# A decode block of attention and gated ReLU: gating before the up and down rows are loaded, and products moved to VectorE

## Chip, cores and metric

The kernel runs on 1 core of one Trainium2 chip. The metric is the device time of one execution in microseconds, as the median of 3 runs. Everything is in 32-bit floats.

## What is computed

One token `x` of 576 numbers is normalized, and attention over a cache of 8192 positions with 32 heads of 128 is added to a gated feed-forward part, both of the same normalized token. Only `x` is small: K and V are 134 MB each, and each of `wq`, `wo`, `W_gate`, `W_up` and `W_down` is 9.4 or 10.6 MB. Each is used once.

```python
D, H, Sk, Dh, F = 576, 32, 8192, 128, 4608

xn = _layernorm(x, axis=-1)

# attention
q = (xn @ wq).reshape(B, 1, H, Dh).transpose(0, 2, 1, 3)
scores = jnp.einsum("bhqd,bhkd->bhqk", q, k_cache) * (Dh ** -0.5)
p = _softmax(scores, axis=-1)
o = jnp.einsum("bhqk,bhkd->bhqd", p, v_cache)
a = o.transpose(0, 2, 1, 3).reshape(B, 1, H * Dh) @ wo

# gated feed-forward
gate = jnp.einsum("bsd,df->bsf", xn, W_gate)
up = jnp.einsum("bsd,df->bsf", xn, W_up)
gate = gate * (gate > 0)
h = gate * up
b = jnp.einsum("bsf,fd->bsd", h, W_down)

return x + a + b
```

Where a gate is not positive, `h` is zero, and neither that column of `W_up` nor that row of `W_down` has a part in the output. The inputs are drawn from a normal distribution with a fixed seed.

## The kernel before

All weights and the cache pass once through a pool of five buffers, `st`, of up to 32 KB on each of the 128 partitions (`NST`, line 25, and line 34). The helper `stream` (line 40) takes a buffer and issues the load; a load can start when the tile that was in its buffer is used up. Most loads are issued by SyncE (SP); every second K tile is issued by ScalarE (`nc.scalar if i % 2 else nc.sync` in `scores`), so two queues carry K and one carries the rest.

The order of work is the order of the program on each engine:

- Line 47 to 89: constants, the normalized `xn` on one partition, and its transposition onto the partitions by six small products into `px`, copied to `xz`. `xz` and `qz` are zero but for one column in 63, so that a window of 32 columns of them puts a product's result into one chosen row of a 32-row block.
- `project` (line 91) multiplies `xn` by a weight matrix on TensorE, with the matrix as the moving side, in five steps of contraction (line 107). It is used for `wq` before everything else, and the result is turned and copied into `qz`.
- For each of four groups of eight heads (`NG`, `G`): `scores` streams eight K tiles of 4 MB, transposed beforehand, and makes one 128 x 512 tile of scores (line 139). `softmax` (line 143) takes maxima and exponentials and turns the result into `pT`. `values` streams eight V tiles of 4 MB (line 180); for each head, VectorE copies the result out of PSUM (`oc`, line 183), and eight matmul instructions add up its four blocks into one column of `ot` (line 185). At the end of the group `os` gets the group's eight output columns.
- `gate_up` is called in the last group between `softmax` and `values`: `project` for `W_gate`, then the ReLU on VectorE (lines 192 and 193), `project` for `W_up`, the product of both, and its turning into `hh`.
- The end: `rows` multiplies a block of 128 rows of `wo` or `W_down` by a column of `os` or `hh` and adds to `acc` (line 218): 32 blocks of `wo` in four loads of eight, then 36 of `W_down` in loads of 8, 8, 8, 6, 4, 1 and 1. Each block is four products of 144 columns, each into another quarter of the partitions. `x` is added, and the 576 numbers are stored.

A 32-bit matmul of the program is two instructions in the trace, so 16 products of a head count 32.

Of the kernel before, what the change touches and what calls it, by code (L numbers as in the profile page):

```python
# [8 lines left out]

F32 = mybir.dt.float32  # L10
AF = mybir.ActivationFunctionType
ALU = mybir.AluOpType
AX = mybir.AxisListType

P = 128
D = 576
H = 32
SK = 8192
DH = 128
F = 4608  # L20
FC = F // P
G = 8
NG = H // G
EPS = 1e-5
SCALE = DH ** -0.5
NST = 5
Q = D // 4


@with_exitstack  # L30
def tile_block(ctx: ExitStack, tc: tile.TileContext, x, kt, vt, wq, wqt, wg, wu, wgt, wut, wo, wd, out):
    nc = tc.nc
    cp = ctx.enter_context(tc.tile_pool(name="cp", bufs=1))
    st = ctx.enter_context(tc.tile_pool(name="st", bufs=NST))
    wk = ctx.enter_context(tc.tile_pool(name="wk", bufs=2))
    pk = ctx.enter_context(tc.tile_pool(name="pk", bufs=2, space=bass.MemoryType.PSUM))
    pv = ctx.enter_context(tc.tile_pool(name="pv", bufs=1, space=bass.MemoryType.PSUM))
    ps = ctx.enter_context(tc.tile_pool(name="ps", bufs=2, space=bass.MemoryType.PSUM))

    def stream(src, queue=nc.sync):  # L40
        n = src.shape[-1]
        t = st.tile([P, n], F32, tag="st", name="st")
        queue.dma_start(t, src)
        return t


    xr = cp.tile([1, D], F32, name="xr")
    nc.scalar.dma_start(xr, x)
    ident = cp.tile([P, P], F32, name="ident")
    make_identity(nc, ident)  # L50

    hs = cp.tile([P, G], F32, name="hs")
    nc.vector.reduce_sum(hs, ident.rearrange("p (j i t) -> p i j t", j=4, i=G), axis=AX.XY)
    sb = cp.tile([P, 4], F32, name="sb")
    nc.vector.reduce_sum(sb, ident.rearrange("p (j m) -> p m j", j=4)[:, :4, :], axis=AX.X)

    x4 = cp.tile([P, Q], F32, name="x4")
    nc.gpsimd.memset(x4, 0.0)
    nc.scalar.dma_start(x4[0:P:32, :], x.rearrange("o (j q) -> (o j) q", j=4))

    one = cp.tile([1, 1], F32, name="one")
    nc.vector.memset(one, 1.0)
    eps = cp.tile([1, 1], F32, name="eps")
    nc.vector.memset(eps, EPS)
    qz = cp.tile([P, H, 63], F32, name="qz")
    nc.gpsimd.memset(qz, 0.0)
    po = [pv.tile([P, 512], F32, name=f"po{i}") for i in range(2)]
    for t in po:
        nc.vector.memset(t, 0.0)


    sm = cp.tile([1, 8], F32, name="sm")
    xn = cp.tile([1, 6 * P], F32, name="xn")
    sq = cp.tile([1, D], F32, name="sq")
    nc.vector.memset(xn, 0.0)
    nc.vector.reduce_sum(sm[:, 0:1], xr, axis=AX.X)
    nc.vector.tensor_scalar_mul(sm[:, 1:2], sm[:, 0:1], 1.0 / D)
    nc.vector.tensor_scalar(sq, xr, sm[:, 1:2], None, op0=ALU.subtract)
    nc.scalar.activation(xn[:, :D], sq, AF.Square, accum_out=sm[:, 2:3])
    nc.scalar.activation(sm[:, 3:4], sm[:, 2:3], AF.Sqrt, bias=eps, scale=1.0 / D)  # L80
    nc.vector.reciprocal(sm[:, 4:5], sm[:, 3:4])
    nc.vector.tensor_scalar_mul(xn[:, :D], sq, sm[:, 4:5])  # L82
    nc.vector.tensor_copy(xn[:, 704:768], xn[:, 512:576])
    px = ps.tile([P, 8], F32, tag="sm", name="px")
    for a in range(6):
        nc.tensor.matmul(px[:, a:a + 1], xn[:, a * P:(a + 1) * P], one, start=True, stop=True)  # L86
    xz = cp.tile([P, 6, 63], F32, name="xz")
    nc.gpsimd.memset(xz, 0.0)
    nc.vector.tensor_copy(xz[:, :, 31], px[:, :6])

    def project(w, wt, slots, n):

        tt = stream(wt)
        pr = pk.tile([P, 512], F32, tag="pk", name="pr")
        for b in range(slots // 4):
            r = b
            for a in range(5):
                if a % 2 == 0 and a < 4:
                    t = stream(w[b, a // 2])
                for j in range(4):  # L100
                    s = 4 * b + j
                    second = s >= slots // 2
                    if a < 4:
                        col, rhs = a, t[:, (a % 2 * 4 + j) * n:][:, :n]
                    else:
                        col, rhs = 4 + second, tt[:, (s % (slots // 2)) * n:][:, :n]
                    nc.tensor.matmul(pr[32 * j:32 * j + 32, :n], xz[:, col, 31 - r:63 - r], rhs,  # L107
                                     start=(b == 0 and a == 0), stop=(s >= slots - 4 and a == 4))
        return pr

    def turned(rows, n):

        m = n // P
        pt = ps.tile([P, 4, P], F32, tag="sm", name="pt")
        for b in range(m):
            nc.tensor.transpose(pt[:, b, :], rows[:, b * P:(b + 1) * P], ident)  # L116
        return pt


    pq = project(wq, wqt, 8, 512)  # L120
    qr = wk.tile([P, 512], F32, tag="p", name="qr")
    nc.vector.tensor_copy(qr, pq)
    pqt = turned(qr, 512)
    for r in range(2):
        nc.vector.tensor_copy(qz[:, 16 * r:16 * r + 16, 31].rearrange("d (j b) -> d j b", b=4),
                              pqt.rearrange("d b (j r) -> d j b r", r=32)[:, :, :, r])

    os = cp.tile([P, H], F32, name="os")

    def scores(g):  # L130
        s = pk.tile([P, 512], F32, tag="pk", name="s")
        for i in range(G):
            h = G * g + i
            t = stream(kt[h], nc.scalar if i % 2 else nc.sync)
            for u in range(4):
                r = 4 * i + u
                for j in range(4):
                    c = (4 * u + j) * 512
                    nc.tensor.matmul(s[32 * j:32 * j + 32, :], qz[:, h, 31 - r:63 - r], t[:, c:c + 512],  # L139
                                     start=(r == 0), stop=(r == 31))  # L140
        return s

    def softmax(g, s):
# [26 lines left out]
    def values(g, pT, rl):  # L170
        ot = ps.tile([P, G], F32, tag="ot", name="ot", bufs=1)
        for i in range(G):
            h = G * g + i
            o = po[h % 2]
            t = stream(vt[h])
            for u in range(4):
                for j in range(4):
                    row = 32 * j + 4 * i + u
                    c = (4 * u + j) * 512
                    nc.tensor.matmul(o[32 * j:32 * j + 4, :], pT[:, row, :], t[:, c:c + 512],  # L180
                                     start=(u == 0), stop=(u == 3))
            oc = wk.tile([P, 512], F32, name="oc")
            nc.vector.tensor_copy(oc, o)  # L183
            for b in range(4):
                nc.tensor.matmul(ot[:, i:i + 1], oc[:, b * P:(b + 1) * P], sb[:, b:b + 1],  # L185
                                 start=(b == 0), stop=(b == 3))
        nc.vector.tensor_mul(os[:, G * g:G * g + G], ot, rl)

    def gate_up():
        pg = project(wg, wgt, 12, 384)  # L190
        gr = wk.tile([P, 512], F32, tag="p", name="gr")
        nc.vector.tensor_scalar(gr[:, :384], pg[:, :384], 0.0, None, op0=ALU.is_gt)
        nc.vector.tensor_mul(gr[:, :384], gr[:, :384], pg[:, :384])
        pu = project(wu, wut, 12, 384)
        nc.vector.tensor_mul(gr[:, :384], gr[:, :384], pu[:, :384])
        ph = turned(gr, 384)
        hh = cp.tile([P, 3, P], F32, name="hh")
        nc.vector.tensor_copy(hh, ph[:, :3, :])
        return hh

    for g in range(NG):
        s = scores(g)
        pT, rl = softmax(g, s)
        if g == NG - 1:
            hh = gate_up()
        values(g, pT, rl)


    acc = pk.tile([P, 512], F32, tag="pk", name="acc")
    nc.vector.memset(acc[:, :Q], 0.0)  # L210
    total = H + FC
    done = 0

    def rows(t, i, col):
        nonlocal done
        for j in range(4):
            c = i * D + j * Q
            nc.tensor.matmul(acc[32 * j:32 * j + 1, :Q], col, t[:, c:c + Q],  # L218
                             start=(done == 0), stop=(done == total - 1))
        done += 1  # L220

    for b in range(4):
        t = stream(wo[b])
        for i in range(8):
            rows(t, i, os[:, 8 * b + i:8 * b + i + 1])
    f = 0
    for n in (8, 8, 8, 6, 4, 1, 1):
        t = stream(wd[:, f * D:(f + n) * D])
        for i in range(n):
            s, b = divmod(f, 3)  # L230
            r = 32 * (s % 4) + s // 4
            rows(t, i, hh[:, b, r:r + 1])
            f += 1
    res = cp.tile([P, Q], F32, name="res")
    nc.vector.tensor_add(res, acc[:, :Q], x4)
    nc.sync.dma_start(out.rearrange("o (j q) -> (o j) q", j=4), res[0:P:32, :])
# [40 lines left out]
```

## Time and profile before

| | |
|---|---|
| runs | 754.05, 753.93, 753.52 us; median 753.93 us |
| profiled execution, first to last instruction | 751.8 us |
| mean granted TensorE clock | 0.761 |
| read from HBM | 319.16 MB |
| DMA issues of K / V | 32 / 32, 4096 KB each |

No time beyond its span is listed for the profiled execution. In the profile's names PE is TensorE, PEld its weight loads, DVE VectorE, ACT ScalarE, POOL GpSimd, SP SyncE, and a q behind a name is the engine's instruction queue. A row of a group reads: line, engine, operation, result<-operands, shapes, count | busy us, mean ns of one | idle time of the engine just before, and what ended it. A row of the DMA issues reads: result<-source, issuing queue, operation, count, KB of one, and median us from issue to landing. In the list of DMA queues a row has the packets, the MB and the time that the packets took as a share of 16 engines' span. In the chain of waits the work that ended last is followed back from its end.

### The profile page before, as it was taken

The page shows a single profiled execution, that of the slowest core. Times are in us where ns is not written, and L with a number is a line of the kernel's source. Part 1 is how long each engine was busy: PE and PEld are TensorE (multiplying, and loading weights), DVE is VectorE, ACT ScalarE, POOL GpSimd, SP SyncE. Part 2 cuts the span into 40 slices and gives each one's busy share as a digit, 9 for nine tenths or more (in the row PEclk, how much of TensorE's full clock was granted, in tenths as well). Part 3 has the DMA queues.
Part 4 walks back from the last instruction along what each step waited for, and adds up shares of the span by engine and source line. Part 5 has one row for each costly group of instructions (what it writes and reads, how often), then busy time and mean ns, then how long its engine had stood idle before and what let it go on. Part 6 is the DMA issues. An engine that isn't in the chain of part 4 may idle for free.

```text
span 751.8 us, 6828 instructions
## 1 busy us (share of the span) xinstructions
PE 422.7 (56%) x3223; PEld 129.3 (17%) x3223; DVE 40.3 (5%) x87; ACT 8.0 (1%) x14; POOL 2.9 (0%) x9
## 2 busy tenths in 40 slices
PE   4353467663463576636445677443745645766755
PEld 2010012211110121101111222111111211221333
DVE  2000001000000010000000100000000100000000
ACT  1000000000000000000000000000000000000000
POOL 1000000000000000000000000000000000000000
PEclk9677788876776797667686776766867997787777
DMA  9999999999999999999999999999999999999996
GB/s 377 432 445 418 445 418 438 425 436 428 432 432 431 433 427 437 425 439 420 439 425 438 425 437 428 432 432 431 433 428 404 415 429 441 424 440 420 429 426 291
DMA packets 13581, 319.60 MB, mean 425 GB/s; under 512 B 1513, under 2 KB 1521, under 8 KB 1778
## 3 DMA queue, kind: packets, MB, share of 16 engines
q1 hardware_dynamic: 11240, 252.06, 78.4%
q10 hardware_dynamic: 2314, 67.11, 20.8%
q8 instruction: 25, 0.41, 0.2%
q14 instruction: 2, 0.02, 0.0%
HBM read 319.16 MB, written 0.00 MB: 425 GB/s over the span
## 4 chain that ended last, share of the span: by engine, by line
DMA 62%; PE 25%; another core or an unknown queue 10%; DVE 2%; issue 0%; ACT 0%; SPq 0%; ACTq 0%
DMA st<-in_kt 26%; DMA st<-in_vt 24%; PE po L180 10%; PE s L139 10%; DMA st<-in_wo 4%; DMA st<-in_wd 3%; DMA st<-in_wu 2%; DMA st<-in_wg 1%; PE pr L107 1%; PE ot L185 1%; DMA st<-in_wq 1%; PE acc L218 1%; DVE oc L183 1%; PE pt L116 0%
## 5 line engine op out<-in xcount | busy, mean ns | idle before, releaser
L180 PE MATMUL po<-st,pT 128*4 128x512 f32 x1024 | 176.4, 851 | 95.6 <-DMA st<-in_vt 93.7
L139 PE MATMUL s<-st,qz 128*32 128x512 f32 x1024 | 139.8, 708 | 140.3 <-DMA st<-in_kt 140.3
L139 PEld LDWEIGHTS s<-st,qz 128*32 128x32 f32 x1024 | 34.9, 128 | 242.0 <-DMA st<-in_kt 142.8
L180 PEld LDWEIGHTS po<-st,pT 128*4 128x4 f32 x1024 | 29.8, 108 | 213.0 <-issue 114.7
L107 PE MATMUL pr<-st,xz 128*32 128x384 f32 (+1 forms) x320 | 38.1, 603 | 32.2 <-DMA st<-in_wq 14.0
L185 PE MATMUL ot<-sb,oc 128*128 128x1 f32 x256 | 33.7, 253 | 26.3 <-DVE oc L183 26.3
L185 PEld LDWEIGHTS ot<-sb,oc 128*128 128x128 f32 x256 | 31.0, 191 | 58.1 <-DVE oc L183 58.1
L183 DVE COPY oc<-po 128x512 f32<-128x512 f32 x32 | 22.1, 691 | 302.5 <-PE po L180 302.5
L107 PEld LDWEIGHTS pr<-st,xz 128*32 128x32 f32 x320 | 9.9, 120 | 57.5 <-DMA st<-in_wq 17.6
L145 DVE TENSOR_REDUCE mr<-s 128x1 f32<-128x512 f32 x4 | 2.8, 691 | 279.5 <-PE s L139 279.5
L218 PE MATMUL acc<-st,hh 128*1 128x144 f32 x288 | 12.8, 344 | 8.6 <-DMA st<-in_wd 8.6
L218 PE MATMUL acc<-st,os 128*1 128x144 f32 x256 | 12.3, 363 | 5.7 <-DMA st<-in_wo 5.7
L218 PEld LDWEIGHTS acc<-st,hh 128*1 128x1 f32 x288 | 8.1, 98 | 13.5 <-DMA st<-in_wd 10.7
L218 PEld LDWEIGHTS acc<-st,os 128*1 128x1 f32 x256 | 7.4, 102 | 10.0 <-DMA st<-in_wo 4.9
L158 ACT ACTIVATE p<-s,nb 128x512 f32<-128x512 f32 x4 | 2.7, 687 | 506.0 <-DVE nb L155 350.4
L86 PE MATMUL px<-one,xn 1*128 1x1 f32 x12 | 2.7, 349 | 7.4 <-DVE xn L82 7.4
L116 PE MATMUL pt<-ident,p 128*128 128x128 f32 x16 | 3.1, 323 | 3.2 <-ACT p L158 3.2
L86 PEld LDWEIGHTS px<-one,xn 1*128 1x128 f32 x12 | 2.6, 324 | 7.4 <-DVE xn L82 7.4
L147 PE MATMUL pm<-ident,mr 128*1 128x128 f32 x4 | 1.1, 270 | 3.3 <-DVE mr L145 3.3
L161 DVE COPY pT<-pt 128x512 f32<-128x512 f32 x4 | 2.8, 691 | 2.6 <-PE pt L116 2.6
L116 PEld LDWEIGHTS pt<-ident,p 128*128 128x128 f32 x16 | 2.0, 160 | 4.1 <-ACT p L158 4.1
L153 PE MATMUL pb<-one,hr 1*128 1x1 f32 x8 | 1.5, 252 | 2.0 <-DVE hr L151 2.0
(51 smaller groups left out, 28.4 us busy)
## 6 DMA issues: line engine op xcount, KB each, us to landing
st<-in_vt SPq DMA_DIRECT2D x32, 4096.0 KB, 40.0
st<-in_kt SPq DMA_DIRECT2D x16, 4096.0 KB, 46.1
st<-in_kt ACTq DMA_DIRECT2D x16, 4096.0 KB, 27.0
st<-in_wg SPq DMA_DIRECT2D x6, 1536.0 KB, 10.2
st<-in_wu SPq DMA_DIRECT2D x6, 1536.0 KB, 12.2
st<-in_wo SPq DMA_DIRECT2D x4, 2304.0 KB, 34.7
st<-in_wq SPq DMA_DIRECT2D x4, 2048.0 KB, 16.0
st<-in_wd SPq DMA_DIRECT2D x3, 2304.0 KB, 23.2
```

Of the source, the lines that this page charges most:

```text
L86: nc.tensor.matmul(px[:, a:a + 1], xn[:, a * P:(a + 1) * P], one, start=True, stop=True)
L107: nc.tensor.matmul(pr[32 * j:32 * j + 32, :n], xz[:, col, 31 - r:63 - r], rhs, start=(b == 0 and a == 0), stop=(s >= slots - 4 and a == 4))
L116: nc.tensor.transpose(pt[:, b, :], rows[:, b * P:(b + 1) * P], ident)
L139: nc.tensor.matmul(s[32 * j:32 * j + 32, :], qz[:, h, 31 - r:63 - r], t[:, c:c + 512], start=(r == 0), stop=(r == 31))
L145: nc.vector.reduce_max(mr, s, axis=AX.X)
L153: nc.tensor.matmul(pb[:, :1], hr.rearrange("p j i t -> p (j i t)"), one, start=True, stop=True)
L158: nc.scalar.activation(p, s, AF.Exp, bias=nb, scale=SCALE, accum_out=lr)
L161: nc.vector.tensor_copy(pT, pt.rearrange("k b r -> k r b"))
L180: nc.tensor.matmul(o[32 * j:32 * j + 4, :], pT[:, row, :], t[:, c:c + 512], start=(u == 0), stop=(u == 3))
L183: nc.vector.tensor_copy(oc, o)
L185: nc.tensor.matmul(ot[:, i:i + 1], oc[:, b * P:(b + 1) * P], sb[:, b:b + 1], start=(b == 0), stop=(b == 3))
L218: nc.tensor.matmul(acc[32 * j:32 * j + 1, :Q], col, t[:, c:c + Q], start=(done == 0), stop=(done == total - 1))
```

## The change

The matrices are laid out anew on the host. `wq` and `W_gate` come transposed, so that a partition holds whole rows of 576: block s of `wq` is one head, block c of `W_gate` is 128 features. `W_up`, transposed, and `W_down` are set side by side as `ud`, 4608 rows of 1152 floats, one for each feature.

`xn` is now computed on all 128 partitions (`xb`). q and the gate are dot products on VectorE, one instruction for 128 outputs (`dot`), 32 for q and 36 for the gate, both before the first K tile. For each of the 36 columns of features, an indirect DMA issued by GpSimd (`fetch`) reads those rows of `ud` whose index is in bounds; where the gate is not positive the index is put out of bounds. Rows left out keep what the buffer had (zero at first), and are multiplied by a gate of zero. There are three such buffers (`NB`). `ffn` makes 128 numbers of `h` by one dot product on VectorE with the gate as its scale, and four products on TensorE add the `W_down` half to `acc`, which now has a PSUM bank of its own. `between` does one `ffn` and one `fetch`; it is called after each head of `scores`, except the first two, and after each head of `values`, until 36 are done.

`project`, `gate_up`, `px`, `xz` and `hh`'s turning are gone. K tiles are all issued by SP. `wo` is streamed at the end alone, in loads of 8, 8, 8, 4, 2, 1 and 1 heads.

```diff
 NST = 5
+NB = 3
+RQ = 11
+RG = 12
...
-    def stream(src, queue=nc.sync):
+    def stream(src):
         n = src.shape[-1]
         t = st.tile([P, n], F32, tag="st", name="st")
-        queue.dma_start(t, src)
+        nc.sync.dma_start(t, src)
         return t
...
+    xa = cp.tile([P, D], F32, name="xa")
+    nc.scalar.dma_start(xa, x.to_broadcast([P, D]))
...
+    num = cp.tile([P, FC], F32, name="num")
+    nc.gpsimd.iota(num, pattern=[[P, FC]], base=0, channel_multiplier=1, allow_small_or_imprecise_dtypes=True)
...
+    gb = [cp.tile([P, 2 * D], F32, name=f"gb{i}") for i in range(NB)]
+    for t in gb:
+        nc.gpsimd.memset(t, 0.0)
...
+    def dot(rows, dst, scale=1.0):
+        nc.vector.tensor_tensor_reduce(out=jk, in0=rows, in1=xb, scale=scale, scalar=0.0,
+                                       op0=ALU.mult, op1=ALU.add, accum_out=dst)
+
+    for s in range(0, H, RQ):
+        n = min(RQ, H - s)
+        t = stream(wq[:, s * D:(s + n) * D])
+        for i in range(n):
+            dot(t[:, i * D:(i + 1) * D], qz[:, s + i, 31:32])
+    gate = cp.tile([P, FC], F32, name="gate")
+    for s in range(0, FC, RG):
+        t = stream(wg[:, s * D:(s + RG) * D])
+        for i in range(RG):
+            dot(t[:, i * D:(i + 1) * D], gate[:, s + i:s + i + 1])
+
+
+    gr = cp.tile([P, FC], F32, name="gr")
+    nc.vector.tensor_scalar(gr, gate, 0.0, None, op0=ALU.is_gt)
+    nc.vector.tensor_mul(gr, gr, gate)
+    off = cp.tile([P, FC], F32, name="off")
+    nc.vector.tensor_scalar(off, gate, 0.0, float(2 * F), op0=ALU.is_le, op1=ALU.mult)
+    idx = cp.tile([P, FC], I32, name="idx")
+    nc.vector.tensor_add(idx, off, num)
+    hh = cp.tile([P, FC], F32, name="hh")
...
+    def rows(t, i, col):
+        nonlocal done
+        for j in range(4):
+            c = i + j * Q
+            nc.tensor.matmul(acc[32 * j:32 * j + 1, :Q], col, t[:, c:c + Q],
+                             start=(done == 0), stop=(done == total - 1))
+        done += 1
+
+    fetched = 0
+
+    def fetch():
+        nonlocal fetched
+        c = fetched
+        t = gb[c % NB]
+        nc.gpsimd.indirect_dma_start(t, None, ud, bass.IndirectOffsetOnAxis(ap=idx[:, c:c + 1], axis=0),
+                                     bounds_check=F - 1, oob_is_err=False)
+        fetched += 1
+
+    def ffn(c):
+        t = gb[c % NB]
+        dot(t[:, :D], hh[:, c:c + 1], gr[:, c:c + 1])
+        rows(t, D, hh[:, c:c + 1])
...
+    used = 0
+
+    def between():
+        nonlocal used
+        if used < FC:
+            ffn(used)
+            used += 1
+            if fetched < FC:
+                fetch()
...
     def scores(g):
...
-            t = stream(kt[h], nc.scalar if i % 2 else nc.sync)
+            t = stream(kt[h])
...
+            if g > 0 or i > 1:
+                between()
         return s
...
+            between()
         nc.vector.tensor_mul(os[:, G * g:G * g + G], ot, rl)
...
+    for _ in range(NB):
+        fetch()
     for g in range(NG):
         s = scores(g)
         pT, rl = softmax(g, s)
-        if g == NG - 1:
-            hh = gate_up()
         values(g, pT, rl)
...
+    h = 0
+    for n in (8, 8, 8, 4, 2, 1, 1):
+        t = stream(wo[:, h * D:(h + n) * D])
...
+        "wq": c(wq.T.reshape(H, P, D).transpose(1, 0, 2)).reshape(P, H * D),
+        "wg": c(wg.T.reshape(FC, P, D).transpose(1, 0, 2)).reshape(P, FC * D),
+        "ud": c(np.concatenate([wu.T, inputs["B_W_down"]], axis=1)),
+        "wo": c(inputs["A_wo"].reshape(H, P, D).transpose(1, 0, 2)).reshape(P, H * D),
```

More of the change, by code (lines that the diff above doesn't have):

```diff
@@ L10 @@
 F32 = mybir.dt.float32
+I32 = mybir.dt.int32
 AF = mybir.ActivationFunctionType
@@ L26, with tile_block @@
 NST = 5
+NB = 3
+RQ = 11
+RG = 12
 Q = D // 4
 @with_exitstack
-def tile_block(ctx: ExitStack, tc: tile.TileContext, x, kt, vt, wq, wqt, wg, wu, wgt, wut, wo, wd, out):
+def tile_block(ctx: ExitStack, tc: tile.TileContext, x, kt, vt, wq, wg, ud, wo, out):
     nc = tc.nc
@@ L38, in tile_block @@
     ps = ctx.enter_context(tc.tile_pool(name="ps", bufs=2, space=bass.MemoryType.PSUM))
-    def stream(src, queue=nc.sync):
+    def stream(src):
         n = src.shape[-1]
         t = st.tile([P, n], F32, tag="st", name="st")
-        queue.dma_start(t, src)
+        nc.sync.dma_start(t, src)
         return t
-    xr = cp.tile([1, D], F32, name="xr")
-    nc.scalar.dma_start(xr, x)
+    xa = cp.tile([P, D], F32, name="xa")
+    nc.scalar.dma_start(xa, x.to_broadcast([P, D]))
+    x4 = cp.tile([P, Q], F32, name="x4")
+    nc.gpsimd.memset(x4, 0.0)
+    nc.scalar.dma_start(x4[0:P:32, :], x.rearrange("o (j q) -> (o j) q", j=4))
     ident = cp.tile([P, P], F32, name="ident")
     make_identity(nc, ident)
+    num = cp.tile([P, FC], F32, name="num")
+    nc.gpsimd.iota(num, pattern=[[P, FC]], base=0, channel_multiplier=1, allow_small_or_imprecise_dtypes=True)
+    eps = cp.tile([P, 1], F32, name="eps")
+    nc.vector.memset(eps, EPS)
+    one = cp.tile([1, 1], F32, name="one")
+    nc.vector.memset(one, 1.0)
     hs = cp.tile([P, G], F32, name="hs")
@@ L55, in tile_block @@
     nc.vector.reduce_sum(sb, ident.rearrange("p (j m) -> p m j", j=4)[:, :4, :], axis=AX.X)
[L57 to L64, printed above, removed]
     qz = cp.tile([P, H, 63], F32, name="qz")
     nc.gpsimd.memset(qz, 0.0)
+    gb = [cp.tile([P, 2 * D], F32, name=f"gb{i}") for i in range(NB)]
@@ L67, in tile_block @@
+    for t in gb:
+        nc.gpsimd.memset(t, 0.0)
     po = [pv.tile([P, 512], F32, name=f"po{i}") for i in range(2)]
-    for t in po:
+    acc = pv.tile([P, 512], F32, name="acc")
+    for t in po + [acc]:
         nc.vector.memset(t, 0.0)
[L72 to L76, printed above, removed]
+    sm = cp.tile([P, 8], F32, name="sm")
@@ L77, in tile_block @@
+    xb = cp.tile([P, D], F32, name="xb")
+    jk = cp.tile([P, D], F32, name="jk")
+    nc.vector.reduce_sum(sm[:, 0:1], xa, axis=AX.X)
     nc.vector.tensor_scalar_mul(sm[:, 1:2], sm[:, 0:1], 1.0 / D)
-    nc.vector.tensor_scalar(sq, xr, sm[:, 1:2], None, op0=ALU.subtract)
-    nc.scalar.activation(xn[:, :D], sq, AF.Square, accum_out=sm[:, 2:3])
+    nc.vector.tensor_scalar(xb, xa, sm[:, 1:2], None, op0=ALU.subtract)
+    nc.scalar.activation(jk, xb, AF.Square, accum_out=sm[:, 2:3])
     nc.scalar.activation(sm[:, 3:4], sm[:, 2:3], AF.Sqrt, bias=eps, scale=1.0 / D)
@@ L81, in tile_block @@
     nc.vector.reciprocal(sm[:, 4:5], sm[:, 3:4])
[L82 to L109, printed above, removed]
@@ new lines, in tile_block @@
+    nc.vector.tensor_scalar_mul(xb, xb, sm[:, 4:5])
+    def dot(rows, dst, scale=1.0):
[7 more added lines that the diff above has]
+    gate = cp.tile([P, FC], F32, name="gate")
@@ new lines, in tile_block @@
+    nc.vector.tensor_add(idx, off, num)
+    hh = cp.tile([P, FC], F32, name="hh")
+    total = H + FC
+    done = 0
+    def rows(t, i, col):
[13 more added lines that the diff above has]
+        fetched += 1
@@ L117, in turned @@
         return pt
[L120 to L126, printed above, removed]
-    os = cp.tile([P, H], F32, name="os")
+    os = cp.tile([P, H], F32, name="os")
+    used = 0
[6 more added lines that the diff above has]
+                fetch()
     def scores(g):
@@ L186, in values @@
                                  start=(b == 0), stop=(b == 3))
+            between()
         nc.vector.tensor_mul(os[:, G * g:G * g + G], ot, rl)
[L189 to L199, printed above, removed]
+    for _ in range(NB):
+        fetch()
     for g in range(NG):
@@ L203, in tile_block @@
         pT, rl = softmax(g, s)
-        if g == NG - 1:
-            hh = gate_up()
         values(g, pT, rl)
[L209 to L228, printed above, removed]
+    h = 0
+    for n in (8, 8, 8, 4, 2, 1, 1):
+        t = stream(wo[:, h * D:(h + n) * D])
         for i in range(n):
[L230 to L233, printed above, removed]
+            rows(t, i * D, os[:, h:h + 1])
+            h += 1
     res = cp.tile([P, Q], F32, name="res")
@@ L246 @@
     V = inputs["A_v_cache"].reshape(H, P, 64 * DH)
-    def tail(w, n):
-        return c(w[512:].reshape(64, 2, n // 2).transpose(1, 0, 2)).reshape(P, n // 2)
-    def blocks(w, b):
-        n = w.shape[1]
-        return c(w[:512].reshape(2, 2, P, b, n // b).transpose(3, 0, 2, 1, 4)).reshape(b, 2, P, 2 * n // b)
     wq, wg, wu = inputs["A_wq"], inputs["B_W_gate"], inputs["B_W_up"]
@@ L259 @@
         "vt": c(V),
-        "wq": blocks(wq, 2),
-        "wqt": tail(wq, H * DH),
-        "wg": blocks(wg, 3),
-        "wu": blocks(wu, 3),
-        "wgt": tail(wg, F),
-        "wut": tail(wu, F),
-        "wo": c(inputs["A_wo"].reshape(4, 8, P, D).transpose(0, 2, 1, 3)).reshape(4, P, 8 * D),
-        "wd": c(inputs["B_W_down"].reshape(FC, P, D).transpose(1, 0, 2)).reshape(P, FC * D),
+        "wq": c(wq.T.reshape(H, P, D).transpose(1, 0, 2)).reshape(P, H * D),
+        "wg": c(wg.T.reshape(FC, P, D).transpose(1, 0, 2)).reshape(P, FC * D),
+        "ud": c(np.concatenate([wu.T, inputs["B_W_down"]], axis=1)),
+        "wo": c(inputs["A_wo"].reshape(H, P, D).transpose(1, 0, 2)).reshape(P, H * D),
     }
```

## The prediction

> **What bounds the kernel now.** I read the head of the page, the queues and the chain first, then the stages in windows, then the instructions that the change touches. The columns of a window are its length, the busy us of each engine, granted clock, DMA share and GB/s.
>
> ```profile
> span 751.8 us, 6828 instructions
> PE 422.7 (56%) x3223; PEld 129.3 (17%) x3223; DVE 40.3 (5%) x87; ACT 8.0 (1%) x14; POOL 2.9 (0%) x9
> ...
> q1 hardware_dynamic: 11240, 252.06, 78.4%
> q10 hardware_dynamic: 2314, 67.11, 20.8%
> ...
> DMA 62%; PE 25%; another core or an unknown queue 10%; DVE 2%; issue 0%; ACT 0%; SPq 0%; ACTq 0%
> ```
>
> ```profile
> 0.00:2.00 2.00, 0.00 (x0) 0.00 (x0) 1.05 (x4) 0.06 (x1) 1.45 (x8) 1.00 0.44 58
> 2.00:20.00 18.00, 8.95 (x52) 3.98 (x52) 3.26 (x11) 3.58 (x5) 1.48 (x2) 1.00 0.98 416
> ...
> 163.00:231.00 68.00, 36.32 (x248) 9.81 (x248) 2.24 (x4) 0.00 (x0) 0.00 (x0) 0.74 1.00 430
> ...
> 590.00:614.00 24.00, 12.21 (x120) 3.46 (x120) 1.29 (x3) 0.00 (x0) 0.00 (x0) 0.93 1.01 428
> 640.00:700.00 60.00, 40.72 (x248) 12.42 (x248) 4.22 (x7) 0.00 (x0) 0.00 (x0) 0.77 1.00 428
> ...
> 728.00:738.00 10.00, 5.81 (x128) 3.66 (x128) 0.00 (x0) 0.00 (x0) 0.00 (x0) 0.83 1.01 430
> 744.60:747.40 2.80, 2.77 (x52) 1.51 (x47) 0.00 (x0) 0.00 (x0) 0.00 (x0) 0.50 0.58 225
> ```
>
> The two load queues together fill 99.2% of the 16 engines' span, and TensorE is busy for 56%. The rate is the same while K streams (163 to 231), while W_up does (590 to 614), while V does (640 to 700) and while W_down does (728 to 738): 428 to 430 GB/s at a DMA share of 1.00. Only the first 2 us and the last few are poorer. So the span is bytes over 430 GB/s, plus both ends; an engine matters only if it holds buffers back for longer than the five of them cover.
>
> ```profile
> L180 PE MATMUL po<-st,pT 128*4 128x512 f32 x1024 | 176.4, 851 | 95.6 <-DMA st<-in_vt 93.7
> L139 PE MATMUL s<-st,qz 128*32 128x512 f32 x1024 | 139.8, 708 | 140.3 <-DMA st<-in_kt 140.3
> ...
> L185 PE MATMUL ot<-sb,oc 128*128 128x1 f32 x256 | 33.7, 253 | 26.3 <-DVE oc L183 26.3
> ...
> L183 DVE COPY oc<-po 128x512 f32<-128x512 f32 x32 | 22.1, 691 | 302.5 <-PE po L180 302.5
> ...
> L218 PE MATMUL acc<-st,hh 128*1 128x144 f32 x288 | 12.8, 344 | 8.6 <-DMA st<-in_wd 8.6
> ```
>
> A 4096 KB head tile needs 4.19 MB / 430 = 9.75 us of DMA. TensorE needs 139.8/32 = 4.4 us of it for K, and (176.4 + 33.7 + 22.1)/32 = 7.3 us for V with the copy at L183. That leaves 2.5 to 5 us per head, and four more tiles in flight (39 us) before a late head stops the stream.
>
> **Bytes taken out.**
>
> ```profile
> st<-in_wu SPq DMA_DIRECT2D x6, 1536.0 KB, 12.2
> ...
> st<-in_wd SPq DMA_DIRECT2D x3, 2304.0 KB, 23.2
> st<-in_wd SPq DMA_DIRECT2D x1, 1728.0 KB, 21.8
> ...
> st<-in_wut SPq DMA_DIRECT2D x1, 1152.0 KB, 11.8
> st<-in_wd SPq DMA_DIRECT2D x1, 1152.0 KB, 19.2
> ...
> st<-in_wd SPq DMA_DIRECT2D x2, 288.0 KB, 13.2
> ```
>
> W_up is 6 x 1536 + 1152 = 10368 KB, 10.62 MB, and W_down the same. At 428 and 430 GB/s they take 24.8 + 24.7 = **49.5 us** of the stream. The two small loads at the end of W_down are copied by the new end of wo (8, 8, 8, 4, 2, 1, 1 heads), so the tail stays as it is: within 2 us either way, taken as 0.
>
> **Bytes put in.** The inputs of the reference give 2275 positive gates of 4608. A kept row is one row of `ud`, 576 + 576 floats or 4608 B, so 36 gathers move 10.48 MB. No transfer issued by GpSimd and no row of 4608 B is in the trace. From below: the full 430 GB/s, 24.4 us. From above: the last two W_down loads, 288 KB each in rows of 2304 B and alone on the queues, 225 GB/s, 46.6 us. What those did while the engines were busy is in the queues' view of the same 2.8 us.
>
> ```profile
> DMA packets 207, 0.63 MB, mean 225 GB/s; under 512 B 27, under 2 KB 27, under 8 KB 177
> ...
> q1 hardware_dynamic: 206, 0.61, 55.1%
> q8 instruction: 1, 0.02, 2.4%
> ```
>
> 0.63 MB in 57.5% of 2.8 us is 391 GB/s. The low mean came of gaps, and beside K and V another queue's packets fill gaps, so I take 391: **26.8 us**. An engine serves a share of the partitions, and the kept rows do not fall evenly: in sixteenths of eight neighbouring partitions there are 131 to 153, mean 142. Eleven rows too many at 391/16 = 24.4 GB/s are **2.1 us** for the engine that ends last (0 if rows are dealt out evenly). The Trainium skill (DMA: Bandwidth & Descriptors, The descriptor swizzle) deals the partitions out in fours from two places; by that the fullest engine has 159 rows and the term would be 3.2 us.
>
> **The loads of wq, wg and wo** keep their bytes in other pieces. wg ran below the rest:
>
> ```profile
> DMA packets 2129, 24.99 MB, mean 417 GB/s; under 512 B 240, under 2 KB 240, under 8 KB 240
> ...
> DMA packets 974, 10.27 MB, mean 428 GB/s; under 512 B 107, under 2 KB 107, under 8 KB 107
> ```
>
> The first line is 560 to 620 us, the second 590 to 614. Without the second the rest of the first is 14.72 MB in 36 us, 409 GB/s. wg's 10.62 MB at 430 instead of 409 are **-1.2 us**. K, which now comes on SP's queue alone, gets V's rate instead of its own, 428 for 430: 0. On one queue a K load stands behind the one before it, which waits for an earlier buffer; since heads are used up in order, that buffer comes free first, so nothing is late for it.
>
> **The products on VectorE.** TENSOR_TENSOR_REDUCE is not in the trace. The nearest rows:
>
> ```profile
> L76 DVE TENSOR_REDUCE sm<-xr 1x1 f32<-1x576 f32 x1 | 0.7, 682 | 0.0
> ...
> L187 DVE TENSOR_TENSOR os<-ot,rl 128x8 f32<-128x8 f32 x4 | 0.7, 167 | 4.6 <-PE ot L185 4.6
> ...
> L193 DVE TENSOR_TENSOR gr<-gr,pr 128x384 f32<-128x384 f32 x1 | 0.6, 554 | 0.0
> ```
>
> The two products give (554 - 167)/376 = 1.03 ns per element, so 576 take 752 ns; that is also my value, with the reduction's 682 below and the sum of both, 1.43 us (two passes), above. q and gate need 32 + 36 dots. The first wq piece (3.24 MB) is in at 2 + 7.5 = 9.5 us. A dot's 295 KB take 0.69 us to load, so at 0.752 VectorE falls slowly behind and ends gate at 9.5 + 68 x 0.752 = 60.6 us. Loads go into a buffer when the load five before is used up: the fifth K tile needs wg's last one, and must be issued some 2 us before the fourth has landed, at about 87.5 us. With dot time d this costs nothing while 9.5 + 68 d < 85.5, d < 1.12 us: 0 at my value, 97.3 + 9.5 - 85.5 = 21 us at 1.43. What covers it is the five buffers.
>
> The 36 dots of `ffn` run in the DMA's shadow too: in `values` a dot stands on VectorE behind the copy at L183 while TensorE does the eight small products of L185 (33.7/32 = 1.05 us), so the following `rows` (12.8/36 = 0.36 us) find it done. But both engines work in order: if a gather is late, its dot holds up the next copy, its `rows` hold up the next head's matmuls, and these hold the stream's buffer. A gather is asked for three heads ahead, 3 x (4.19 + 0.29)/430 = 31 us. GpSimd does nothing else by then, and the first use comes after the third K tile.
>
> **At the end** only wo (9.44 MB, 22 us) follows V, and all its products wait for the last head.
>
> ```profile
> 701.23 6.30 PE L180 MATMUL po<-st,pT 128*4 128x512 f32 x32 [1.80 <-DMA st<-in_vt]
> ...
> 709.33 2.14 PE L218 MATMUL acc<-st,os 128*1 128x144 f32 x64
> ...
> 717.90 4.02 PE L218 MATMUL acc<-st,os 128*1 128x144 f32 x64 [3.54 <-DMA st<-in_wo]
> ```
>
> They start 8.1 us after the last V tile. 28 heads in chunks of 8 at 2.14 us (at 4.02 on a low clock) are done 15.6 to 22.2 us after it, when the last pieces land: 0, up to 2 us more.
>
> **The sum** is 751.8 - 49.5 + 26.8 + 2.1 - 1.2 = 730.0 us of span. The median of the runs, 753.93, stands 2.1 above the span, so **732 us**.
>
> **Rivals.**
>
> *The gathers run at the rate of a lone small load.* Then they take 46.6 instead of 26.8 us, 752 us: no change. For it: a load of 288 KB alone left the engines idle for 42%. Against it: where two queues were open they shared the engines without a gap, in the queues' view of 548 to 568 us:
>
> ```profile
> q10 hardware_dynamic: 153, 4.49, 52.4%
> q1 hardware_dynamic: 150, 4.11, 47.7%
> ```
>
> The Trainium skill (DMA: Bandwidth & Descriptors, Anatomy of one DMA — SWDGE (gpsimd) path) gives a transfer issued by GpSimd about 2.0 us fixed beside its bytes; were 36 of those paid in the open, an estimate from that page adds 72 us and gives about 804. No run here shows it yet. In between lies a dearer row, 733 to 752 us.
>
> *A gather comes back too late (slower).* The place is `between`: the dot waits, TensorE behind it, the buffers behind that. If the way from request to landing and back takes 40 us, as the median of a V load does,
>
> ```profile
> st<-in_vt SPq DMA_DIRECT2D x32, 4096.0 KB, 40.0
> ```
>
> a head of the first 36 takes 13.3 instead of 10.4 us, 105 us of lag, less the 39 us of tiles in flight: 732 + 66 = 798 us. It costs something from 39/36 + 10.4 = 11.5 us per head, 34.5 us there and back, and more than the gain from 36.3 us. For it: one queue more behind deep ones. Against it: 40 us is the depth of SP's own queue, four tiles; GpSimd's is another, the two queues above took turns about evenly, and an engine's eight rows behind eight 32 KB packets (32 KB at 430/16 GB/s, 1.22 us) are 8 x (1.22 + 0.19) = 11 us.
>
> *The skipped rows are moved after all,* or cost their engines the same: 21.2 MB at 391 are 54.3 us, no unevenness, 757 us.
>
> *A dot is two passes:* 732 + 21 = 753 us.
>
> **Chances.** Forecast 0.67 (725 to 740: gathers at 430 and even, a tail better by 2 us, at the low end; at the high end some 8 us of dearer rows, unevenness and end). Dear rows or lone rate 0.12, two thirds of it faster by over 0.2%. Two passes 0.03, no change. Late gather 0.10, fixed price in the open 0.04, skipped rows moved 0.04: slower. A measurement of this kernel cannot tell under 0.2% (1.5 us) from no change. Faster 0.67 + 0.08 = 0.75, same 0.04 + 0.03 = 0.07, slower 0.10 + 0.04 + 0.04 = 0.18. The range takes in the dear rows: 725 to 752.
>
> **What would show it.** Right: queues q1 plus GpSimd's near 99% again, 308 MB, some 430 GB/s through K and V, PE's waits at L139 and L180 still for DMA, dots under 0.8 us, gathers landing within 30 us. Wrong: windows under 420 GB/s in the first 400 us but not later (dear rows), PE idle on VectorE's hh with SP waiting for PE (late gather), 319 MB read (rows not skipped), DMA gaps around 85 us (dots too slow).

## The result and the profile after

The changed kernel takes 778.62 us (median of 4 runs, 778.14 to 779.29) against 753.91 us before: a ratio of 1.0326, 95% interval 1.0311 to 1.0341. It is slower, where 732 us had been forecast.

The head of its page and its queues:

```profile
span 776.4 us, 6505 instructions
...
DMA  9999987767769999999999999999999999999996
...
q1 hardware_dynamic: 11096, 297.93, 89.9%
q0 software_dynamic: 5184, 10.49, 4.1%
...
DMA 71%; PE 15%; DVE 10%; issue 2%; ACT 1%; POOLq 0%; POOL 0%; DVEq 0%; ACTq 0%
```

The bytes are those of the prediction: GpSimd's queue, q0, moved 10.49 MB, and the whole 309 MB. But the DMA engines, full in nearly every slice before,

```profile
DMA  9999999999999999999999999999999999999996
```

have a hollow now from the sixth slice to the twelfth, some 100 to 235 us. The windows of that stretch (columns as in the prediction):

```profile
60.00:100.00 40.00, 6.96 (x40) 1.68 (x40) 12.79 (x37) 0.00 (x0) 4.10 (x4) 0.63 1.01 433
100.00:150.00 50.00, 14.75 (x152) 4.09 (x152) 8.81 (x22) 0.00 (x0) 10.87 (x11) 0.64 0.75 293
150.00:200.00 50.00, 16.75 (x164) 4.41 (x168) 10.93 (x27) 0.00 (x0) 12.78 (x12) 0.64 0.72 274
200.00:250.00 50.00, 30.93 (x269) 9.12 (x265) 11.97 (x30) 0.78 (x2) 11.14 (x9) 0.72 0.79 305
250.00:300.00 50.00, 37.28 (x292) 12.85 (x281) 5.00 (x8) 0.00 (x0) 0.00 (x0) 0.89 1.01 433
```

From 100 to 250 us the stream ran at 291 GB/s on average instead of 430, a loss of 150 x (1 - 291/430) = 48 us. Later it is at its old rate. With the 309.13 MB at 430 GB/s and the 8.5 us that the ends took before (751.8 us less 319.60 MB at that rate), these 48 us make up the span of 776.4 us to within 1 us. So the time went into one stretch, the one in which GpSimd (fifth number) is busy. The costliest groups there, with what each engine waited for:

```profile
L123 PE MATMUL acc<-gb,hh 128*1 128x144 f32 x288 | 18.9, 354 | 115.0 <-DVE hh L92 114.9
...
L92 DVE CUSTOM_DVE_ANT_0 jk<-st,xb 128x576 f32<-128x576 f32 x68 | 51.5, 757 | 2.3
L133 POOL DMA_INDIRECT gb<-in_ud,idx x36 | 38.9, 1080 | 181.1 <-PE acc L123 73.1
L92 DVE CUSTOM_DVE_ANT_0 jk<-gb,xb,gr 128x576 f32<-128x576 f32 x36 | 29.5, 819 | 128.5 <-DMA gb<-in_ud,idx 128.1
...
gb<-in_ud,idx POOLq DMA_INDIRECT x36, 11.5
```

A dot takes 757 ns, as forecast (752). But TensorE waited 115 us for `hh`, VectorE 128 us for gathers. The gather took a median of 11.5 us to land, much less than the 34.5 us from which one block per head would have cost time. The timeline of TensorE shows why it cost time all the same:

```profile
89.83 0.66 PE L123 MATMUL acc<-gb,hh 128*1 128x144 f32 x8 [21.75 <-DVE hh L92]
100.61 0.66 PE L123 MATMUL acc<-gb,hh 128*1 128x144 f32 x8 [10.13 <-DVE hh L92]
111.42 0.66 PE L123 MATMUL acc<-gb,hh 128*1 128x144 f32 x8 [10.14 <-DVE hh L92]
114.74 0.66 PE L123 MATMUL acc<-gb,hh 128*1 128x144 f32 x8 [2.67 <-DVE hh L92]
115.17 5.21 PE L169 MATMUL s<-st,qz 128*32 128x512 f32 x32
120.21 1.12 PE L123 MATMUL acc<-gb,hh 128*1 128x144 f32 x24
```

Eight instructions are one block of `rows`. Four blocks stand between the first K tile and the second. The same timeline, read on to 231 us, gives the place of all 36: after these four, there are 5, 6, 6, 6, 6 and 3 blocks between the following K tiles, and the last is done before the eighth head of the first group. The fourth block came only 3.3 us after the third because the stream had stopped by then: from 111 to 119 us the load queue q1 moved 0.03 MB.

The program calls `between` once per head over 36 heads, but a planner, a part of the compiler, sorts the instructions of each engine before they run, and here it put the blocks far ahead of their places in the program; by what reckoning, no run shows. What the text ahead of the prediction says, that the order of work is the order of the program on each engine, is wrong. The trace of before had shown it, on a small scale. This is its chain of waits in the last group, where `project` for the gate stands in the program behind the whole softmax:

```profile
582.39 0.27 PE pm L147
582.66 0.78 PE pr L107 x6
583.43 0.31 PE pb L153 x2
583.74 1.41 PE pr L107 x10
585.15 0.59 PE pt L116 x4
```

The first products of the gate (L107) ran inside the softmax (L147, L153, L116).

### The profile page after: what moved, and what is told of

Read it like the earlier page. It is cut to its first block, busy times and chain, and to the rows that moved or that the text cites. A ratio compares the mean times of both kernels' runs of the same rounds, so it can differ in the third digit from the quotient of the medians.

```text
span 776.4 us, 6505 instructions
## 1 busy us (share of the span) xinstructions
PE 408.0 (53%) x2884; PEld 117.6 (15%) x2884; DVE 118.7 (15%) x289; ACT 8.0 (1%) x14; POOL 44.6 (6%) x48
## 2 busy tenths in 40 slices
DMA packets 16460, 309.13 MB, mean 398 GB/s; under 512 B 4166, under 2 KB 4174, under 8 KB 6961
## 3 DMA queue, kind: packets, MB, share of 16 engines
q0 software_dynamic: 5184, 10.49, 4.1%
HBM read 319.46 MB, written 0.00 MB: 411 GB/s over the span
## 4 chain that ended last, share of the span: by engine, by line
DMA 71%; PE 15%; DVE 10%; issue 2%; ACT 1%; POOLq 0%; POOL 0%; DVEq 0%; ACTq 0%
DMA st<-in_kt 33%; DMA st<-in_vt 16%; DMA gb<-in_ud,idx 15%; DVE jk L92 8%; PE po L212 7%; PE s L169 6%; DMA st<-in_wo 6%; DMA xa<-in_x 2%; PE acc L123 1%; PE ot L217 1%; DVE oc L215 0%; PE pt L146 0%; ACT p L190 0%; DVE mr L177 0%; DVE pT L193 0%
## 5 line engine op out<-in xcount | busy, mean ns | idle before, releaser
L169 PE MATMUL s<-st,qz 128*32 128x512 f32 x1024 | 176.6, 852 | 154.6 <-DMA st<-in_kt 154.6
L212 PE MATMUL po<-st,pT 128*4 128x512 f32 x1024 | 164.7, 802 | 52.7 <-DMA st<-in_vt 50.4
L169 PEld LDWEIGHTS s<-st,qz 128*32 128x32 f32 x1024 | 40.9, 150 | 282.6 <-DMA st<-in_kt 113.0
L123 PE MATMUL acc<-gb,hh 128*1 128x144 f32 x288 | 18.9, 354 | 115.0 <-DVE hh L92 114.9
L92 DVE CUSTOM_DVE_ANT_0 jk<-st,xb 128x576 f32<-128x576 f32 x68 | 51.5, 757 | 2.3
L133 POOL DMA_INDIRECT gb<-in_ud,idx x36 | 38.9, 1080 | 181.1 <-PE acc L123 73.1
L92 DVE CUSTOM_DVE_ANT_0 jk<-gb,xb,gr 128x576 f32<-128x576 f32 x36 | 29.5, 819 | 128.5 <-DMA gb<-in_ud,idx 128.1
L123 PEld LDWEIGHTS acc<-gb,hh 128*1 128x1 f32 x288 | 4.5, 81 | 131.1 <-DVE hh L92 128.2
L73 POOL MEMSET gb<- 128x1152 f32 x3 | 3.0, 1047 | 0.0
L92 DVE DVE_READ_ACCUMULATOR2_ANT hh<- 128x1 f32 x36 | 3.0, 82 | 0.0
## 6 DMA issues: line engine op xcount, KB each, us to landing
gb<-in_ud,idx POOLq DMA_INDIRECT x36, 11.5
```

Of the source, the lines that this page charges most:

```text
L73: nc.gpsimd.memset(t, 0.0)
L92: nc.vector.tensor_tensor_reduce(out=jk, in0=rows, in1=xb, scale=scale, scalar=0.0, op0=ALU.mult, op1=ALU.add, accum_out=dst)
L133: nc.gpsimd.indirect_dma_start(t, None, ud, bass.IndirectOffsetOnAxis(ap=idx[:, c:c + 1], axis=0), bounds_check=F - 1, oob_is_err=False)
```

## Experiments

Each ratio is against runs of the kernel before that were made along with the experiment (medians of 753.8 to 754.2 us).

First theory (A): the planner's order makes 36 gathers follow one another in front of seven K tiles, and each is slow beside the stream because packets of two queues take turns on an engine. The gathers landed 10.8 us apart (89.83, 100.61, 111.42 above). The two queues from 78 to 88 us:

```profile
DMA packets 281, 4.37 MB, mean 437 GB/s; under 512 B 90, under 2 KB 90, under 8 KB 157
...
q1 hardware_dynamic: 140, 4.06, 94.7%
q0 software_dynamic: 141, 0.31, 7.9%
```

One packet of the gather for one of the stream, 141 to 140, although one is 4.6 KB or less and the other 32 KB. And 90 of these packets are under 512 B. In all, q0 has 5184 packets, 36 x (128 + 16): 16 for completion and 128 rows per gather. The page counts 4166 packets under 512 B, and 1833 where all rows are gathered (e3, the second line):

```profile
DMA packets 16460, 309.13 MB, mean 398 GB/s; under 512 B 4166, under 2 KB 4174, under 8 KB 6961
DMA packets 16460, 319.87 MB, mean 404 GB/s; under 512 B 1833, under 2 KB 1841, under 8 KB 6961
```

The difference is 2333, the number of rows left out. A skipped row is still a packet, of 4 bytes, and takes its turn. Eight rows and a completion behind 1.22 us each are 11 us. The Trainium skill (DMA: Bandwidth & Descriptors, Queues, rings and completion order) has an engine go round its queues packet by packet, and calls 9 to 17 descriptors typical for a packet. The trace agrees with the turns, 141 to 140, but here a turn was a single row: a gather has nine packets on an engine, and took nine turns.

### e1: one block per head, tied on TensorE

```diff
+                    last = nc.tensor.matmul(s[...])
...
             if g > 0 or i > 1:
-                between()
+                with tc.issue_after(last.ins):
+                    between()
```

The same stands in `values` behind the last product into `ot`. `issue_after` holds the instructions of the block that run on the engine of `last`, TensorE, behind it; the dots run on VectorE.

> The changed kernel, but the four products of each feature block are tied behind the last product of their own head, so that one block is used per head, over 36 heads, instead of all 36 in the first group. Theory A (the planner put all 36 in front of the first seven K tiles, TensorE waits there for gathers that follow each other too slowly, and the stream stops when its five buffers are full): the windows hold 430 GB/s from 100 to 240 us too, 728 to 738 us. In the changed kernel three gathers asked for at once landed 10.8 us apart beside the stream, and a head takes 10.4 us, so a lag of about 0.4 us per head may build up (14 us over 36 heads), which the tiles in flight cover. Rival B (the gathers burden the stream itself wherever they stand): the same 45 us are lost, only thinner, 770 us or more, with windows under 420 GB/s up to some 440 us.

Measured: 791.04 us, ratio 1.0481 (1.0453 to 1.0510). Neither theory had this. VectorE's timeline after the first group's scores:

```profile
163.33 0.82 DVE L92 CUSTOM_DVE_ANT_0 jk<-gb,xb,gr 128x576 f32<-128x576 f32 x1 [9.48 <-DMA gb<-in_ud,idx]
...
173.80 0.82 DVE L92 CUSTOM_DVE_ANT_0 jk<-gb,xb,gr 128x576 f32<-128x576 f32 x1 [7.22 <-DMA gb<-in_ud,idx]
174.55 0.69 DVE L194 COPY pT<-pt 128x512 f32<-128x512 f32 x1
...
199.66 0.82 DVE L92 CUSTOM_DVE_ANT_0 jk<-gb,xb,gr 128x576 f32<-128x576 f32 x1 [17.10 <-DMA gb<-in_ud,idx]
200.40 0.69 DVE L216 COPY oc<-po 128x512 f32<-128x512 f32 x1
```

The dots were not tied, and the planner moved them ahead on VectorE: in front of the softmax, and in front of the copy of a head's result. There the copy waits 17 us for a gather that was asked for only after the products before it. While the blocks stood behind their own heads, from 60 to 200 us, the windows held 427 to 432 GB/s, so rival B (a burden on the stream wherever the gathers stand) falls too; e5 and e6 below have the same gathers and no hollow. The second theory, A2: what costs time is work that holds buffers standing behind gathers, on either engine.

### e2: rows of 8 KB in the stream

```diff
+        m = n // parts
+        for k in range(parts):
+            nc.sync.dma_start(t[:, k * m:(k + 1) * m], src[:, k * m:(k + 1) * m])
...
-            t = stream(kt[h])
+            t = stream(kt[h], 4 if g == 0 else 1)
```

and the same for `vt`.

> The changed kernel with its order, but the K and V tiles of the first group are loaded in four pieces each, in rows of 8 KB instead of 32 KB. Theory A with its mechanism (the gather's packets, skipped rows among them, take turns one by one with the stream's packets on each engine: nine turns of 1.22 us are 11 us; turns of 8 KB take 0.31 us by the 8 KB rows of wqt before): a gather beside the stream lands in 3 to 5 us, 36 of them end near 200 us instead of 240, and the stream loses under 15 us: 732 to 748 us. Rival C (what takes 11 us is GpSimd's or the gather's own, whatever the stream's packets): landing stays at 11 us and the time at 770 to 785 us.

Measured: 755.34 us, 1.0011 (0.9998 to 1.0024), 23 us less than the changed kernel. The first dots on VectorE:

```profile
81.78 0.82 DVE L94 CUSTOM_DVE_ANT_0 jk<-gb,xb,gr 128x576 f32<-128x576 f32 x1 [9.57 <-DMA gb<-in_ud,idx]
85.28 0.82 DVE L94 CUSTOM_DVE_ANT_0 jk<-gb,xb,gr 128x576 f32<-128x576 f32 x1 [2.68 <-DMA gb<-in_ud,idx]
88.87 0.82 DVE L94 CUSTOM_DVE_ANT_0 jk<-gb,xb,gr 128x576 f32<-128x576 f32 x1 [2.76 <-DMA gb<-in_ud,idx]
```

A gather every 3.5 us instead of 10.8, for the same three gathers, asked for at the same time: the length of a turn is the stream's packet. Rival C is out. The time itself tells less, since the planner's order changed too (one or two blocks now stand behind each quarter of a K tile). The expected range was missed by 7 us: the blocks still held the first group's scores until 203 us, against 137 us without them (e4), and the windows from 100 to 150 and 150 to 200 us fell to 379 and 289 GB/s, a loss of 22 us where under 15 had been expected.

### e3: all rows gathered, planner's order

```diff
-    nc.vector.tensor_add(idx, off, num)
+    nc.vector.tensor_copy(idx, num)
```

> The changed kernel, but no index is put out of bounds, so that all 4608 rows are gathered; the rows with a gate of zero are multiplied by zero, the output is the reference's. Theory A: a skipped row takes its turn all the same (2909 packets of 4 bytes on GpSimd's queue are 576 for completion and 2333 for skipped rows), so 10.75 MB more land partly in the time that the stream stands still: landings 11 to 14 us, 780 to 800 us. Rival C (a gather's time goes with the rows it moves): gathers take about twice as long, 36 of them some 150 us more, over 850 us. If the skip bought its full bytes, the time would be 778.6 + 25 = 804 us.

Measured: 795.12 us, 1.0544 (1.0519 to 1.0568). The first three gathers no longer wait for the gate, and the planner put their blocks in front of the first K tile, at 72 to 75 us; otherwise the order is much like the changed kernel's. The next three dots:

```profile
91.09 0.82 DVE L92 CUSTOM_DVE_ANT_0 jk<-gb,xb,gr 128x576 f32<-128x576 f32 x1 [16.23 <-DMA gb<-in_ud,idx]
102.22 0.82 DVE L92 CUSTOM_DVE_ANT_0 jk<-gb,xb,gr 128x576 f32<-128x576 f32 x1 [10.31 <-DMA gb<-in_ud,idx]
113.35 0.82 DVE L92 CUSTOM_DVE_ANT_0 jk<-gb,xb,gr 128x576 f32<-128x576 f32 x1 [10.30 <-DMA gb<-in_ud,idx]
```

11.1 us apart with twice the bytes, against 10.8 with half of the rows skipped. Beside the stream a gather's pace goes by its rows, kept or not.

### e4: no feed-forward part

```diff
-    total = H + FC
+    total = H
...
-        if used < FC:
+        if used < 0:
...
-    for _ in range(NB):
-        fetch()
```

> Leaves out the gathers, their dot products and the W_down products: the output has attention and x alone. q and gate on VectorE, K on one queue and wo at the end stay. 298.6 MB at 430 GB/s and 5 us at the ends: 698 to 706 us if those parts cost nothing beside the stream, as the prediction had it. With e1 it gives the price of the gathers in the stream, predicted as 26.8 + 2.1 us. Rival D (a part of the 46 us lost comes from the dots before K, the broadcast of x, the single K queue or the new end): 715 us or more.

Measured: 704.93 us, 0.9345 (0.9329 to 0.9362). Its 298.58 MB at 430 GB/s leave 8.5 us of its span of 702.9 us for the ends, as before. So the dots for q and gate, the broadcast of `x`, K on one queue and the new end cost nothing beside the stream. The whole loss lies in the 36 blocks: 778.6 - 704.9 = 74 us for what was forecast at 28.9.

### e5 and e6: the dots tied too, and the blocks spread

```diff
+            copied = nc.vector.tensor_copy(oc, o)
...
+    def between(last):
+        nonlocal used, place
+        place += 1
+        if used < FC * place // 62:
+            with ExitStack() as after:
+                after.enter_context(tc.issue_after(last.ins))
+                if copied is not None:
+                    after.enter_context(tc.issue_after(copied.ins))
+                ffn(used)
```

e5 has one block per head, without `place`; e6 is as shown. The blocks of the first group's scores have no copy in front of them (`copied` is None); they are tied on TensorE alone.

> As e1, and each dot product on VectorE is also tied behind the last copy of a head's result (oc), so that none stands in front of the softmax or of an earlier copy. Theory A2 (a gather beside the 32 KB stream takes nine turns, 10.8 us; e1 lost its time where dots of later blocks stood ahead of the softmax and of the copies on VectorE and these waited for gathers): 36 gathers at 10.8 us against heads of 10.4 us leave a lag of 0.4 to 1 us per head, 14 to 36 us, which the 39 us of tiles in flight just cover: 732 to 750 us. Rival B2 (the pace of the gathers alone, wherever the dots stand): 775 us or more, as e1.

> As e5, with the 36 blocks spread over all 62 places, one for 1.72 heads or 17.9 us of stream. Theory A2: nothing waits any more, the gathers' bytes alone are paid: 704.9 of e4 + 10.48 MB at 391 GB/s (26.8 us) + up to 2 us = 731 to 735 us, faster than both kernels. Rival B2 (gathers cost the stream more than bytes, by their 4-byte packets or unevenness): 740 us or more, with windows under 425 GB/s.

Measured: e5 734.34 us, 0.9742 (0.9726 to 0.9758); e6 734.34 us, 0.9737 (0.9721 to 0.9753). Both are 2.6% faster than before. The windows of e5 over the old hollow:

```profile
100.00:150.00 50.00, 28.05 (x185) 7.46 (x189) 6.61 (x17) 0.78 (x2) 4.92 (x5) 0.77 1.01 428
150.00:200.00 50.00, 34.03 (x248) 10.08 (x244) 7.50 (x15) 0.00 (x0) 4.92 (x5) 0.77 1.01 429
200.00:250.00 50.00, 31.89 (x220) 8.47 (x212) 6.28 (x14) 0.00 (x0) 3.94 (x4) 0.77 1.00 427
```

Its gathers land a median of 29.8 us after they are asked for:

```profile
gb<-in_ud,idx POOLq DMA_INDIRECT x36, 29.8
```

and 15.7 us in e6; both are later than the 11.5 us of the changed kernel, and neither stops the stream. VectorE even waited longer for gathers in e5 than in the changed kernel (128.1 us):

```profile
DVE jk L92 <- DMA gb<-in_ud,idx: 231.8, 34, 16.7
```

So at these landing times it is not the wait that costs, but how much work that frees the stream's buffers stands behind it. The upper estimate of e5's lag did not come: the tiles in flight covered it all, and spreading the blocks bought nothing more.

### e7: e6 with all rows

> As e6, but all 4608 rows are gathered; rows with a gate of zero are multiplied by zero. Theory A2: with no wait left, the 10.75 MB cost their bytes, 25 to 28 us over e6: 756 to 763 us, the time of before or a little more. Rival (the skipped rows cost as much as rows that move): within 5 us of e6.

Measured: 756.57 us, 1.0037 (1.0023 to 1.0051). The skip is worth 756.57 - 734.34 = 22.2 us, near the 25 us of its 10.75 MB, once nothing waits; in the planner's order (e3 less the changed kernel, with three blocks placed otherwise) it was worth 16.5. Without it the rebuilt kernel would be a little slower than before.

### e8: plain loads on ScalarE's queue

```diff
-        nc.gpsimd.indirect_dma_start(t, None, ud, bass.IndirectOffsetOnAxis(ap=idx[:, c:c + 1], axis=0),
-                                     bounds_check=F - 1, oob_is_err=False)
+        nc.scalar.dma_start(t, ud[c * P:(c + 1) * P, :])
```

> The changed kernel with its planner's order (36 blocks in the first group), but each gather is a plain load of all 128 rows of ud, issued by ScalarE on its own queue. Theory A (turns of packets between queues, whoever issues): a load beside the 32 KB stream lands 10 to 12 us after the one before, and the time is 775 to 800 us, near e3. Rival C (GpSimd's way of issuing, or the indirection, is what is slow): loads in 3 us, no stall: 752 to 760 us.

Measured: 787.75 us, 1.0449 (1.0429 to 1.0470), from two runs. Its loads land in 12.3 us at the median, its windows fall to 349 and 328 GB/s. As in e3, three blocks stand in front of the first K tile. The fifth and sixth dots:

```profile
89.01 0.82 DVE L92 CUSTOM_DVE_ANT_0 jk<-gb,xb,gr 128x576 f32<-128x576 f32 x1 [10.32 <-DMA gb<-in_ud]
91.75 0.82 DVE L92 CUSTOM_DVE_ANT_0 jk<-gb,xb,gr 128x576 f32<-128x576 f32 x1 [1.92 <-DMA gb<-in_ud]
```

The first came beside the stream, 11 us after the dot before it; the next four came 1.4 to 2.7 us apart, while the stream stood still (0.03 MB on its queue from 90 to 98 us). Neither the indirection nor GpSimd is what is slow; a row-wise load on a second queue beside the stream is.

### e9: only the dots tied

The line with `last.ins` is taken out of e5.

> As e5, but only the dot products are tied (behind the last copy of a head's result on VectorE); the products on TensorE are where the planner puts them: six blocks in front of the third head of the first group, seven more around the first head of the second. Theory A2 (what stops the stream is a queue of gathers at 10.8 us each in front of work that holds buffers): six gathers in a row are some 60 us against two heads' time of 20, so about 40 us of lag, just over what the tiles in flight cover, then again up to 40: 740 to 765 us, between e5 (734) and the changed kernel (778). Rival (VectorE's order alone decides): 732 to 737 us, as e5.

Measured: 755.51 us, 1.0015 (1.0002 to 1.0028), as A2 had it, between both. By TensorE's timeline six blocks stand in front of the third K tile, eight around the first head of the second group and six around the first head of the third, and the windows show three hollows, each following one of these places:

```profile
100.00:150.00 50.00, 30.22 (x260) 8.18 (x264) 3.64 (x10) 0.00 (x0) 4.93 (x5) 0.74 0.87 358
150.00:200.00 50.00, 34.44 (x233) 10.28 (x225) 8.07 (x19) 0.78 (x2) 3.95 (x4) 0.74 1.01 430
200.00:250.00 50.00, 25.21 (x192) 7.62 (x184) 7.47 (x17) 0.00 (x0) 6.13 (x6) 0.70 1.01 428
250.00:300.00 50.00, 15.00 (x128) 5.05 (x132) 4.96 (x12) 0.00 (x0) 5.93 (x6) 0.60 0.87 355
...
450.00:550.00 100.00, 62.45 (x441) 17.84 (x441) 6.80 (x15) 0.78 (x2) 0.00 (x0) 0.74 0.91 390
```

The blocks have to be held in place on both engines.

## Why the prediction was wrong

**The bound: right.** Bytes over 430 GB/s, and an engine matters only if it holds buffers back longer than four tiles cover. e4 to e7 follow that sum; the changed kernel is the case of the second half of the sentence.

**Bytes out and in: right, for a kernel in program order.** With the order kept, the gathers cost 734.34 - 704.93 = 29.4 us; 26.8 + 2.1 had been the terms; neither was tried by itself. The whole sum said 732, e5 and e6 give 734.34. The 2.0 us per transfer of the Trainium skill (DMA: Bandwidth & Descriptors, Anatomy of one DMA — SWDGE (gpsimd) path) are not paid in the open here: by an estimate from that page 36 of them would have been 72 us more.

**The products on VectorE: right in the end, wrong on the way.** The dots began at 17.3 us, not 9.5, because the broadcast of `x` landed 11.7 us after its issue and the normalization came behind it, and they follow at 0.80 us (757 ns and a read of the accumulator that partly overlaps), not 0.752. The gate ended at 71.7 us instead of 60.6. The five buffers covered that, as e4 shows.

**The step that failed** is "A gather is asked for three heads ahead, 3 x (4.19 + 0.29)/430 = 31 us", with "the first use comes after the third K tile". Both took the calls in the program for the order of the engines. The planner set the first use after the first K tile, at 89.8 us, and up to six blocks between two heads. A gather was still asked for three blocks ahead, but three blocks no longer lay three heads apart: the one issued at 120.94 us, for example, was wanted at once. VectorE waited 13.1 us for it and TensorE 13.5 us for `hh`, with the next K tile's products behind. Where the program's order was forced (e5), the 31 us were right: gathers landing in 29.8 us cost nothing.

**The rival that came true** is the late gather, given 0.10. Its place was right (the dot waits, TensorE behind it, the buffers behind that). Its price was worked out for one block per head, and so asked for a landing beyond 34.5 us, against which the 11 us of turns, correctly worked out, seemed harmless. The 11 us are not only a delay: beside the stream, queued gathers follow each other at that pace. With all 36 in the first group, its softmax began at 234 us, against 137 us without them (e4) and 143 us with one block per head (e5), and the 39 us in flight cannot cover 98 us.

**"Skipped rows are moved after all"** was half true: not their bytes (q0 moved 10.49 MB), but their turns.

**A sign that was none:** the 319 MB read that were to show unskipped rows. The page's line of HBM reads says 319.46 MB for the changed kernel, and also for e3, whose queues moved 319.87 MB instead of 309.13. Only the packets tell.

## What to carry to other kernels

Before you price work that the program scatters between other work, find out from the trace, or the compiled order, where a planner has put it; a few instructions ahead of their place in the trace of before are warning enough. Where a product waits for a slow load, tie it behind the work that frees the stream's buffers on every engine that it runs on, or that work will wait too. A load of many short rows beside a stream of long ones went at the pace of the stream's packets here, so count its rows per engine, skipped ones too, and not only its bytes.

## What the runs showed of the hardware that was not expected

- While both had work, two queues got through the same number of packets, whatever their sizes: 141 and 140 in 10 us, with 4.6 KB or less against 32 KB. With 8 KB rows in the stream a gather of 128 rows came every 3.5 us instead of every 10.8.
- A row left out by the bounds of an indirect DMA is still a packet: 2333 packets of 4 bytes for 2333 rows.
- The broadcast of `x`, 288 KB in 128 rows on ScalarE's queue, took 11.7 us to land beside the 25 KB rows of `wq`. Nine turns of 0.94 us (25344 B at 430/16 GB/s) would be 8.5 us of it, by an estimate; that was not tried by itself.
